# Attention and two expert layers in one kernel: bias moved behind the gather, smaller pieces at the ends of the routing and of the last expert

## Chip, cores and metric

The kernel runs on one core of one Trainium2 chip. The metric is the device time of one execution in microseconds (us). The engines are TensorE (PE in the rows; PEld is its weight load), VectorE (DVE), ScalarE (ACT), GpSimd (POOL) and SyncE (SP), which issues most DMAs. Each engine works through its own queue in order.

## What is computed

The reference, cut to what matters here: an attention over 4 batches and 8 heads with two sparse masks, a dense layer with a squared relu, and a mixture of 8 experts in which every expert gets 288 of the 2304 tokens.

```python
x = attn(q, k, v)                          # 2304 x 512
h = np.maximum(x @ w_in, 0.0)              # 2304 x 2048
x2 = (s * (h * h) + b) @ w_out             # 2304 x 512
logits = x2 @ w_gate                       # 2304 x 8
...                                        # greedy: 288 tokens to each expert
for e in range(8):
    u = np.maximum(x2[mask_e] @ w1[e], 0.0)
    out[mask_e] = u @ w2[e]
```

The scalar bias b reaches x2 as b times the column sums of w_out, one number for each of the 512 columns and the same for every token.

## The kernel before

All matmuls of the dense and expert layers run in a three-pass split: an operand is cut into a high part (a cast) and a low part (what the cast left over), and high x high, high x low and low x high are summed in PSUM.

`mix1` (L590) runs the attention and the first dense layer. Squared relus go to DRAM (`ud`) and come back later. `load_out` (L465) loads w_out, sums its rows in `acc`, and at the end makes from it, with one matmul by ones and one ScalarE activation (L481, L482), a tile `acc` of 128x512 that holds the bias in every partition.

The second dense layer is `x2_late` (L722). It yields after every matmul of 512 columns (L731), so that other code can take them one at a time as filling. `late_step` (L680) loads a block, casts it on ScalarE (L700), subtracts on VectorE (L703) and puts its matmuls into a queue; when a group of 384 tokens is done, `x2_row` (L551) takes each block of 128 tokens out of PSUM with one VectorE operation, which multiplies by s and adds the bias tile (L555), and writes the row to `x2d` in DRAM (L556). There are 18 such rows. The last one is kept apart: its 48 matmuls (`self.tail`, L952) run after the routing.

`route` (L782) finds the experts' tokens in seven rounds of small VectorE steps and small matmuls. Each `yield n` in it lets `run` (L1091) issue n late matmuls before the next step; the numbers are the constants FA0, FA, FB, FP, FC, FK and FE. At the end it builds one-hot tiles (`o96` by L906, `o24` by L908, `w24` by L910 and L911) and gets from 36 small matmuls (L916) the token indices `idx` (L920).

`first_gather` (L940) fetches the first expert's 288 rows with three indirect DMAs on GpSimd, computes meanwhile the last 128 tokens, transposes the rows on TensorE (L958) and adds to them, by a matmul with a "hot" matrix (L963), those rows that only exist in SBUF as yet. `put_x` (L968) then takes one chunk of 96 tokens (four blocks of 96 columns, one for each 128 of the 512 columns, all in one PSUM tile) to `X`: the high part by ScalarE (L971), the low part by VectorE (L972). `gather` (L974) does the same for each later expert: a chunk's DMA in one step, its transposes (L986) three steps later, `put_x` one step after that.

`run` goes through the experts in eight steps each. In a step TensorE runs the second layer (L1023) of the step before last and the first layer (L998) of this step; ScalarE does the relu of the last step (L1004) and two weight casts (L386); VectorE does the relu's low part (L1005) and two weight subtractions (L388). The chunks of the next expert are put in steps 5, 6 and 7, after these. At the end of an expert come the last weight casts and three subtractions, and only then the relu of step 7.

`last_expert` (L1053) computes its second layer token by token (three chunks of 96 tokens, 24 matmuls of 512 columns each, L1061) and writes each chunk with `put`: half a copy on ScalarE (L1067), half on VectorE (L1068), and an indirect DMA on GpSimd to the output (L1069).

Of the kernel before, what the change touches and what calls it, by code (L numbers as in the profile page):

```python
# [74 lines left out]
class Body:  # L75
# [27 lines left out]
    FE = (4, 14, 20)  # L103
# [361 lines left out]
    def load_out(self, fc):  # L465
# [10 lines left out]
        if fc == 15:  # L476
            yield
            yield
            yield
            ps = self.ps()  # L480
            nc.tensor.matmul(ps, self.onesf, self.acc, start=True, stop=True)  # L481
            nc.scalar.activation(self.acc, ps, AF.Copy, scale=self.sb[:, 1:2])  # L482
# [68 lines left out]
    def x2_row(self, g, t, acc):  # L551
# [3 lines left out]
        nc.vector.scalar_tensor_tensor(_two(row), _nat(acc[t]), self.sb[:, 0:1], _two(self.acc), op0=ALU.mult, op1=ALU.add)  # L555
# [226 lines left out]
    def route(self):  # L782
# [66 lines left out]
        for rnd in range(7):  # L849
# [56 lines left out]
        tt(o96, pm.unsqueeze(2).to_broadcast([128, 18, 96]), self.iotaf.unsqueeze(1).to_broadcast([128, 18, 96]),  # L906
           op=ALU.is_equal)
# [4 lines left out]
        yield self.FE[2]  # L912
# [7 lines left out]
        nc.vector.tensor_copy(self.idx, ip[:96, :24])  # L920

# [18 lines left out]
    def first_gather(self):  # L940
# [13 lines left out]
        pss = []  # L954
        for c in range(3):
            ps = self.ps()
            for dc in range(4):
                nc.tensor.matmul(ps[:, dc * 96:(dc + 1) * 96], rows[c][:, dc * 128:(dc + 1) * 128], self.identf[:96, :96],  # L958
                                 start=(dc == 0), stop=False, is_transpose=True, skip_group_check=True)
            pss.append(ps)  # L960
        for c in range(3):
            for dc in range(4):
                nc.tensor.matmul(pss[c][:, dc * 96:(dc + 1) * 96], last[:, dc * 128:(dc + 1) * 128], hot[:, c, :],  # L963
                                 start=False, stop=(dc == 3), skip_group_check=True)
            self.put_x(X, c, pss[c])
        return X

    def put_x(self, X, c, ps):  # L968
        v = ps[:, :384].rearrange("p (d t) -> p d t", d=4)
        h = X[:, 0, :, c * 96:(c + 1) * 96]  # L970
        self.nc.scalar.copy(h, v)  # L971
        self.nc.vector.tensor_tensor(X[:, 1, :, c * 96:(c + 1) * 96], v, _f(h), op=ALU.subtract)  # L972

    def gather(self, e):  # L974
# [3 lines left out]
        def one(c):  # L978
# [9 lines left out]
            self.put_x(X, c, ps)  # L988
# [64 lines left out]
    def last_expert(self, e, X, w1, w2):  # L1053
# [19 lines left out]

        def step(fc):
# [7 lines left out]
            if fc == 7:  # L1082
                put(0)
                for c in (1, 2):
                    for f in range(8):
                        layer2(f, c)
                    put(c)
# [107 lines left out]
```

## Time and profile before

| | us |
|---|---|
| three timed runs, median | 750.45 |
| lowest, highest | 744.54, 750.58 |
| the profiled execution | 745.06 |
| its span, first to last instruction | 743.3 |
| busy in it: TensorE, VectorE, ScalarE, GpSimd | 720.1, 497.9, 374.5, 56.5 |

The profile shows one execution. A row of a timeline gives an instruction's start, its duration, engine, line, output and inputs, and in brackets how long the engine sat idle before it and what released it. Pipelined instructions overlap a little, so the next can start before the recorded end of the last. Attention and the first layer take the first 310 us or so, the second dense layer and the routing go on until 527, the experts until the end.

### The profile page before, as it was taken

What the parts mean: (1) busy time and instruction counts of PE and PEld (TensorE: products, weight loads), DVE (VectorE), ACT (ScalarE), POOL (GpSimd) and SP (SyncE); (2) the same over time, 40 slices, a digit from 0 to 9 for tenths busy, and PEclk for the clock granted to TensorE, in tenths of its full rate; (3) what the DMA queues carried; (4) which work ended last, traced back from release to release, by engine and by line L of the source; (5) the groups of instructions that cost most, each with busy time, mean ns of one, the idle gap of its engine ahead of it and who ended that gap; (6) DMA issues with size and microseconds to landing.
All of it is one profiled execution on the core that took longest, in us unless ns stands there. A gap on an engine that the chain in (4) does not pass through costs nothing.

```text
span 743.3 us, 16623 instructions
## 1 busy us (share of the span) xinstructions
PE 720.1 (97%) x6276; PEld 643.6 (87%) x6276; DVE 497.9 (67%) x1222; ACT 374.5 (50%) x893; POOL 56.5 (8%) x81
## 2 busy tenths in 40 slices
PE   8979999999999999999999998999999999999996
PEld 6769999999999877788778777878999999999994
DVE  6899997987551344478798878794466565666620
ACT  4888776677775655532414221220355555555520
POOL 4000000000000000000000000001112211321211
PEclk9989999999999999999999999999999999999999
DMA  8967756875885899634344423351857767756411
GB/s 234 292 205 224 224 168 210 256 242 193 275 296 192 265 299 296 194 118 154 145 137 148 158 88 117 96 160 60 250 188 236 216 169 239 225 182 191 138 33 32
DMA packets 84655, 140.17 MB, mean 189 GB/s; under 512 B 10848, under 2 KB 44384, under 8 KB 84576
## 3 DMA queue, kind: packets, MB, share of 16 engines
q1 hardware_dynamic: 81504, 129.68, 55.2%
q0 software_dynamic: 3072, 9.44, 3.9%
q8 instruction: 49, 0.80, 0.5%
q14 instruction: 30, 0.25, 0.1%
HBM read 106.32 MB, written 32.77 MB: 187 GB/s over the span
## 4 chain that ended last, share of the span: by engine, by line
PE 82%; DVE 12%; DMA 2%; issue 2%; ACT 0%; SPq 0%; POOLq 0%; DVEq 0%
PE b L501 22%; PE b L731 18%; PE b L998 13%; PE b L1023 11%; PE b L258 2%; PE b L538 2%; PE b L326 2%; PE b L1061 1%; PE b L952 1%; PE b L1039 1%; DVE u L703 1%; DMA r<-ud 1%; PE b L424 1%; DVE wl L388 1%; DVE W L409 1%
## 5 line engine op out<-in xcount | busy, mean ns | idle before, releaser
L731 PE MATMUL b<-wh,u 128*128 128x512 f32 x544 | 168.4, 390 | 1.1 <-DVE u L703 1.1
L731 PEld LDWEIGHTS b<-wh,u 128*128 128x128 f32 x544 | 98.0, 190 | 14.6 <-DVE u L703 1.8
L700 ACT CAST u<-r 128x384 fp32r<-128x384 f32 (+1 forms) x96 | 46.3, 493 | 126.7 <-DMA r<-ud 61.5
L731 PE MATMUL b<-wl,u 128*128 128x512 f32 x272 | 103.3, 380 | 0.0
L1023 PE MATMUL b<-u,wh 128*128 128x288 f32 x448 | 87.9, 293 | 0.0
L501 PE MATMUL b<-xh,wh 128*128 128x384 f32 x384 | 84.0, 341 | 1.1 <-ACT xh L368 1.1
L388 DVE TENSOR_TENSOR wl<-raw,wh 128x512 fp32r<-128x512 f32 x128 | 82.9, 683 | 0.4
L501 PE MATMUL b<-xl,wh 128*128 128x384 f32 x384 | 79.0, 328 | 1.0 <-DVE xl L369 1.0
L386 ACT CAST wh<-raw 128x512 fp32r<-128x512 f32 x128 | 73.3, 618 | 11.1 <-DVE u L703 11.1
L501 PE MATMUL b<-xh,wl 128*128 128x384 f32 x384 | 78.8, 328 | 0.0
L506 ACT ACTIVATE r<-b 128x384 f32<-128x384 f32 x96 | 47.1, 490 | 62.5 <-PE b L501 61.3
L998 PE MATMUL b<-X,wh 128*128 128x288 f32 x512 | 73.4, 286 | 0.6 <-ACT X L971 0.6
L501 PEld LDWEIGHTS b<-xh,wh 128*128 128x128 f32 x384 | 63.0, 191 | 8.7 <-PE b L538 3.1
L1023 PEld LDWEIGHTS b<-u,wh 128*128 128x128 f32 x448 | 69.4, 189 | 0.0
L998 PEld LDWEIGHTS b<-X,wh 128*128 128x128 f32 x512 | 67.4, 189 | 1.3 <-ACT X L971 0.7
L1005 DVE SCALAR_TENSOR_TENSOR u<-b,u 128x288 fp32r<-128x288 f32 x64 | 29.2, 456 | 57.9 <-ACT u L1004 44.6
L501 PEld LDWEIGHTS b<-xl,wh 128*128 128x128 f32 x384 | 65.5, 191 | 1.3 <-DVE xl L369 1.3
L501 PEld LDWEIGHTS b<-xh,wl 128*128 128x128 f32 x384 | 65.4, 190 | 0.2 <-DVE wl L388 0.2
L1023 PE MATMUL b<-u,wl 128*128 128x288 f32 x224 | 64.1, 286 | 0.0
L703 DVE TENSOR_TENSOR u<-r,u 128x384 fp32r<-128x384 f32 (+1 forms) x96 | 47.9, 527 | 15.7 <-ACT u L700 15.6
L731 PEld LDWEIGHTS b<-wl,u 128*128 128x128 f32 x272 | 51.4, 189 | 7.3
L507 ACT ACTIVATE r<-r 128x384 f32<-128x384 f32 x96 | 50.5, 526 | 3.0
(207 smaller groups left out, 1106.4 us busy)
## 6 DMA issues: line engine op xcount, KB each, us to landing
raw<-in_moe_w_dram SPq DMA_DIRECT2D x128, 256.0 KB
r<-ud SPq DMA_DIRECT2D x160, 192.0 KB
ud<-r SPq DMA_DIRECT2D x96, 192.0 KB
raw<-in_words_dram SPq DMA_DIRECT2D x64, 256.0 KB
qk<-in_q_dram SPq DMA_DIRECT2D x24, 288.0 KB
x2d<-E SPq DMA_DIRECT2D x18, 256.0 KB
wod<-K SPq DMA_DIRECT2D x16, 256.0 KB
wo<-wod SPq DMA_DIRECT2D x16, 256.0 KB
```

The lines of the kernel that those rows point to most:

```text
L258: nc.tensor.matmul(sp[64 * j:64 * j + p, c * kw:(c + 1) * kw], qk[sl, 0, q0:q0 + p], qk[sl, 1, k0:k0 + kw], start=after, stop=after or c = ...
L386: nc.scalar.copy(h, W)
L388: nc.vector.tensor_tensor(l, W, _f(h), op=ALU.subtract)
L501: nc.tensor.matmul(ps[:, :self.G], w[:, dc * 128:(dc + 1) * 128], _alt(self.xg[g][dc][x]), start=(k == 0), stop=(k == 11))
L506: nc.scalar.activation(_two(r), _nat(ps[:, :self.G]), AF.Relu)
L507: nc.scalar.activation(r, r, AF.Square)
L700: nc.scalar.copy(d[0], src)
L703: nc.vector.tensor_tensor(d[1], src, _f(d[0]), op=ALU.subtract)
L731: self.nc.tensor.matmul(**args)
L998: self.nc.tensor.matmul(ps[:, :288], w1[dc, fh][wi][:, fs:fs + 128], _alt(X[:, xi, dc, :]), start=(k == 0), stop=(k == 11))
L1005: self.nc.vector.scalar_tensor_tensor(_two(l), _nat(ps[:, :288]), 0.0, _two(_f(h)), op0=ALU.max, op1=ALU.subtract)
L1023: nc.tensor.matmul(y[dc][:, :288], w[:, sl], _alt(u[:, j, :288]), start=(fc == 0 and i == 0), stop=(fc == 7 and i == 2))
```

## The change

- `x2_row` copies on ScalarE, scaled by s, without the bias. `load_out` makes the bias as a tile of 128x4 (a column for each 128 of the 512), by four matmuls of one column.
- `put_x` handles one block of columns and adds the bias there: on ScalarE as the activation's pointer bias, on VectorE as the pointer scalar of a three-operand operation. `gather` calls it four times for a chunk.
- `first_gather` keeps one PSUM tile for each block of 128 columns and 288 tokens in place of one for each chunk of 96 tokens, so the "hot" matmuls are four of 288 columns, and `put_x` takes a quarter of X at a time.
- In `route` the one-hot tile is built in two halves, with five late matmuls issued before each half and before the next tile, and nine before the index matmuls: 24 in place of 20. Two more index columns, `idx2`, address the output in half rows.
- In `last_expert` the third chunk is computed and written in two halves of 256 columns.

```diff
--- before.py
+++ after.py
@@ -100,7 +100,7 @@
     P1S = 28
     A2S = 8
     TM = 2
-    FE = (4, 14, 20)
+    FE = (4, 14, 5, 9)
     P0S = 20
     H0 = (36, 38)
     AE = 2
@@ -478,8 +478,11 @@
             yield
             yield
             ps = self.ps()
-            nc.tensor.matmul(ps, self.onesf, self.acc, start=True, stop=True)
-            nc.scalar.activation(self.acc, ps, AF.Copy, scale=self.sb[:, 1:2])
+            for dc in range(4):
+                nc.tensor.matmul(ps[:, dc:dc + 1], self.acc[:, dc * 128:(dc + 1) * 128], self.onesf[:, :1], start=True,
+                                 stop=True, skip_group_check=True)
+            self.bias = self.c.tile([128, 4], F32, name="bias")
+            nc.scalar.activation(self.bias, ps[:, :4], AF.Copy, scale=self.sb[:, 1:2])
 
     def prep_end(self):
         nc = self.nc
@@ -552,7 +555,7 @@
         nc = self.nc
         i = g * 3 + t
         row = self.Es[i % self.NE].rearrange("p c k -> p (c k)")
-        nc.vector.scalar_tensor_tensor(_two(row), _nat(acc[t]), self.sb[:, 0:1], _two(self.acc), op0=ALU.mult, op1=ALU.add)
+        nc.scalar.activation(_two(row), _nat(acc[t]), AF.Copy, scale=self.sb[:, 0:1])
         nc.sync.dma_start(self.x2d[i * 128:(i + 1) * 128, :], row)
         return row
 
@@ -903,13 +906,17 @@
         stt(pm, ao, -96.0, po, op0=ALU.mult, op1=ALU.add)
         stt(cm, eo, 3.0, ao, op0=ALU.mult, op1=ALU.add)
         o96 = self.xf.tile([128, 18, 96], BF, tag="xb", name="o96")
-        tt(o96, pm.unsqueeze(2).to_broadcast([128, 18, 96]), self.iotaf.unsqueeze(1).to_broadcast([128, 18, 96]),
-           op=ALU.is_equal)
+        for h in range(2):
+            yield self.FE[2]
+            r = slice(9 * h, 9 * h + 9)
+            tt(o96[:, r], pm[:, r].unsqueeze(2).to_broadcast([128, 9, 96]), self.iotaf.unsqueeze(1).to_broadcast([128, 9, 96]),
+               op=ALU.is_equal)
+        yield self.FE[2]
         tt(o24, cm.unsqueeze(2).to_broadcast([128, 18, 24]),
            self.iotaf[:, :24].unsqueeze(1).to_broadcast([128, 18, 24]), op=ALU.is_equal)
         ts(w24[:, 0], o24, self.iotap, None, op0=ALU.mult)
         tt(w24[:, 1], o24, self.iotat.unsqueeze(2).to_broadcast([128, 18, 24]), op=ALU.mult)
-        yield self.FE[2]
+        yield self.FE[3]
         ip = self.ps()
         for i in range(18):
             for k in range(2):
@@ -918,6 +925,9 @@
         self.o96, self.o24 = o96, o24
         self.idx = c.tile([96, 24], I32, name="idx")
         nc.vector.tensor_copy(self.idx, ip[:96, :24])
+        self.idx2 = c.tile([96, 2], I32, name="idx2")
+        for h in range(2):
+            ts(self.idx2[:, h:h + 1], ip[:96, 23:24], 2.0, float(h), op0=ALU.mult, op1=ALU.add)
 
 
     def prep2(self, e, w1, w2):
@@ -951,25 +961,22 @@
         for args in self.tail:
             nc.tensor.matmul(**args)
         last = self.x2_row(self.NG - 1, 2, self.xacc[self.NG - 1])
-        pss = []
-        for c in range(3):
-            ps = self.ps()
-            for dc in range(4):
-                nc.tensor.matmul(ps[:, dc * 96:(dc + 1) * 96], rows[c][:, dc * 128:(dc + 1) * 128], self.identf[:96, :96],
-                                 start=(dc == 0), stop=False, is_transpose=True, skip_group_check=True)
-            pss.append(ps)
+        pss = [self.ps() for _ in range(4)]
         for c in range(3):
             for dc in range(4):
-                nc.tensor.matmul(pss[c][:, dc * 96:(dc + 1) * 96], last[:, dc * 128:(dc + 1) * 128], hot[:, c, :],
-                                 start=False, stop=(dc == 3), skip_group_check=True)
-            self.put_x(X, c, pss[c])
+                nc.tensor.matmul(pss[dc][:, c * 96:(c + 1) * 96], rows[c][:, dc * 128:(dc + 1) * 128], self.identf[:96, :96],
+                                 start=(c == 0), stop=False, is_transpose=True, skip_group_check=True)
+        for dc in range(4):
+            nc.tensor.matmul(pss[dc][:, :288], last[:, dc * 128:(dc + 1) * 128], hot.rearrange("p c t -> p (c t)"),
+                             start=False, stop=True, skip_group_check=True)
+            self.put_x(X, dc, 0, pss[dc][:, :288])
         return X
 
-    def put_x(self, X, c, ps):
-        v = ps[:, :384].rearrange("p (d t) -> p d t", d=4)
-        h = X[:, 0, :, c * 96:(c + 1) * 96]
-        self.nc.scalar.copy(h, v)
-        self.nc.vector.tensor_tensor(X[:, 1, :, c * 96:(c + 1) * 96], v, _f(h), op=ALU.subtract)
+    def put_x(self, X, dc, t, v):
+        h, l = (X[:, i, dc, t:t + v.shape[1]] for i in range(2))
+        bias = self.bias[:, dc:dc + 1]
+        self.nc.scalar.activation(h, v, AF.Identity, bias=bias)
+        self.nc.vector.scalar_tensor_tensor(l, v, bias, _f(h), op0=ALU.add, op1=ALU.subtract)
 
     def gather(self, e):
         nc = self.nc
@@ -985,7 +992,8 @@
             for dc in range(4):
                 nc.tensor.transpose(ps[:, dc * 96:(dc + 1) * 96], t[:, dc * 128:(dc + 1) * 128], self.identf[:96, :96])
             yield
-            self.put_x(X, c, ps)
+            for dc in range(4):
+                self.put_x(X, dc, c * 96, ps[:, dc * 96:(dc + 1) * 96])
 
         return X, (one(c) for c in range(3))
 
@@ -1071,6 +1079,18 @@
                 out_offset=bass.IndirectOffsetOnAxis(ap=self.idx[:, 3 * e + c:3 * e + c + 1], axis=0),
                 in_=t, in_offset=None)
 
+        def half(h):
+            ps = self.ps()
+            for f in range(8):
+                for i, (j, w) in enumerate(((0, 0), (0, 1), (1, 0))):
+                    nc.tensor.matmul(ps[:96, :256], us[f][j][:, 192:288], _alt(w2[f][w][:, 256 * h:256 * h + 256]),
+                                     start=(f == 0 and i == 0), stop=(f == 7 and i == 2))
+            t = self.wt([96, 256], F32, "yh")
+            nc.scalar.copy(_two(t), _nat(ps[:96, :256]))
+            nc.gpsimd.indirect_dma_start(
+                out=self.a["out"].rearrange("n (h d) -> (n h) d", h=2),
+                out_offset=bass.IndirectOffsetOnAxis(ap=self.idx2[:, h:h + 1], axis=0), in_=t, in_offset=None)
+
         def step(fc):
             ps = self.layer1(fc, X, w1)
             yield
@@ -1081,10 +1101,11 @@
             layer2(fc, 0)
             if fc == 7:
                 put(0)
-                for c in (1, 2):
-                    for f in range(8):
-                        layer2(f, c)
-                    put(c)
+                for f in range(8):
+                    layer2(f, 1)
+                put(1)
+                half(0)
+                half(1)
 
         return (step(fc) for fc in range(8))
```

VectorE at the end of the routing, from the last small step on. `o` is the one-hot tile, `u` and `ul` are low parts that the late matmuls need. Before:

```order
L903 SCALAR_TENSOR_TENSOR rt<-rt 128x18
L904 SCALAR_TENSOR_TENSOR rt<-rt 128x18
L906 TENSOR_TENSOR o_6992<-rt,iotaf 128x1728
L908 TENSOR_TENSOR rt<-rt,iotaf 128x432
L910 TENSOR_SCALAR rt<-rt,iotap 128x432
L911 TENSOR_TENSOR rt<-rt,iotat 128x432
L703 TENSOR_TENSOR u_6975<-r_6948,u_6975 128x256
L703 TENSOR_TENSOR ul_6976<-r_6948,ul_6976 128x128
L703 TENSOR_TENSOR u_7001<-r_6965,u_7001 128x256
L703 TENSOR_TENSOR ul_7002<-r_6965,ul_7002 128x128
```

After:

```order
L907 SCALAR_TENSOR_TENSOR rt<-rt 128x18
L706 TENSOR_TENSOR u_6979<-r_6952,u_6979 128x256
L706 TENSOR_TENSOR ul_6980<-r_6952,ul_6980 128x128
L912 TENSOR_TENSOR o_6996<-rt,iotaf 128x864
L706 TENSOR_TENSOR u_7001<-r_6969,u_7001 128x256
L706 TENSOR_TENSOR ul_7002<-r_6969,ul_7002 128x128
L912 TENSOR_TENSOR o_6996<-rt,iotaf 128x864
L915 TENSOR_TENSOR rt<-rt,iotaf 128x432
L917 TENSOR_SCALAR rt<-rt,iotap 128x432
L918 TENSOR_TENSOR rt<-rt,iotat 128x432
```

The four subtractions (L703, now L706) stood behind the whole one-hot work; now two stand ahead of its first half and two between the halves, and the index work is behind all of them.

ScalarE where an expert ends: two weight casts, the last chunk of the next expert's X, two more weight casts, the relu of step 7. In brackets is whose count an instruction waits for. Before:

```order
L1004 ACTIVATE u_1360_7452<-b_7408 128x288 [waits DVE_49,PE_49]
L386 CAST wh_7469<-raw_1355_7425 128x512 [waits DMAHW2_49]
L386 CAST wh_7475<-raw_1358_7431 128x512 [waits DMAHW3_49,DVE_49]
L971 CAST X_7210<-b_7435 128x4x96 [waits PE_49]
L386 CAST wh_7483<-raw_1364_7472 128x512 [waits DMAHW4_49]
L386 CAST wh_7487<-raw_1367_7478 128x512 [waits DMAHW5_49]
L1004 ACTIVATE u_1372_7503<-b_7455 128x288 [waits DVE_49,PE_49]
```

After:

```order
L1012 ACTIVATE u_1361_7467<-b_7417 128x288 [waits PE_49,Activation_49]
L386 CAST wh_7484<-raw_1356_7434 128x512 [waits DMAHW2_49]
L386 CAST wh_7490<-raw_1359_7440 128x512 [waits DMAHW3_49,Activation_49]
L978 ACTIVATE X_7213<-b_7450,bias 128x96 [waits PE_49]
L978 ACTIVATE X_7213<-b_7450,bias 128x96 [waits DVE_49] x3
L386 CAST wh_7504<-raw_1365_7487 128x512 [waits DMAHW4_49]
L386 CAST wh_7508<-raw_1368_7493 128x512 [waits DMAHW5_49]
L1012 ACTIVATE u_1373_7524<-b_7470 128x288 [waits PE_49,Activation_49]
```

One piece that waits for the transposes became four: the first waits for the transposes, each of the other three for VectorE's work on the piece before it.

GpSimd at the end of the program: scatters of finished rows; DMASW is the landing of an earlier scatter or gather. Before:

```order
L1045 DMA out_dram<-yr_9894,idx 2304x512 [waits DMASW2_49,DVE_49]
L1045 DMA out_dram<-yr_9922,idx 2304x512 [waits DMASW4_49,DMASW3_49,Activation_49]
L1069 DMA out_dram<-E_129,idx 2304x512 [waits DMASW4_49,DVE_49]
L1069 DMA out_dram<-E_130,idx 2304x512 [waits DMASW6_49,DMASW5_49,DVE_49]
L1069 DMA out_dram<-E_131,idx 2304x512 [waits DMASW6_49,DVE_49]
```

After:

```order
L1053 DMA out_dram<-yr_10051,idx 2304x512 [waits DMASW4_49,DMASW3_49,Activation_49]
L1077 DMA out_dram<-E_129,idx 2304x512 [waits DMASW4_49,DVE_49]
L1077 DMA out_dram<-E_130,idx 2304x512 [waits DMASW6_49,DMASW5_49,DVE_49]
L1090 DMA out_dram<-yh_10200,idx_7075 4608x256 [waits DMASW6_49,Activation_49]
L1090 DMA out_dram<-yh_10228,idx_7075 4608x256 [waits DMASW7_49,DMASW0_49,Activation_49]
```

One scatter more; each waits, besides its own data, for the landing of the scatter ahead of it.

## Rows read from the trace of the kernel before

**Rows 1.** The page's line of engines: busy us (share of the span) and instructions.

```profile
PE 720.1 (97%) x6276; PEld 643.6 (87%) x6276; DVE 497.9 (67%) x1222; ACT 374.5 (50%) x893; POOL 56.5 (8%) x81
```

**Rows 2.** Busy us of each engine between 600 and 700 us; PE clock, DMA share, GB/s.

```profile
600.00:700.00 100.00, 100.00 (x835) 100.00 (x834) 61.84 (x116) 54.99 (x120) 23.03 (x23) 1.00 0.66 201
```

**Rows 3.** TensorE's waits, 300 to 530 us: total us, times, longest.

```profile
PE b L868 <- DVE rt L862: 3.1, 2, 2.1
PE b L874 <- DVE jc L872: 1.3, 3, 0.7
...
PE b L731 <- DVE u L703: 1.1, 1, 1.1
PE b L998 <- ACT X L971: 0.6, 1, 0.6
```

**Rows 4.** Timeline of VectorE, 446 to 458 us: start, us, instruction [idle before].

```profile
447.82 1.41 DVE L555 SCALAR_TENSOR_TENSOR E<-b,sb,acc 128x512 f32<-128x512 f32 x2 [0.38 <-PE b L731]
...
451.24 0.74 DVE L555 SCALAR_TENSOR_TENSOR E<-b,sb,acc 128x512 f32<-128x512 f32 x1
```

**Rows 5.** Timeline of the routing's end, 503 to 512 us.

```profile
504.63 1.96 DVE L906 TENSOR_TENSOR o<-rt,iotaf 128x1728 bf16<-128x1728 bf16 x1
...
507.39 0.60 DVE L911 TENSOR_TENSOR rt<-rt,iotat 128x432 bf16<-128x432 bf16 x1
...
508.38 0.70 PE L731 MATMUL b<-wh,u 128*128 128x512 f32 x2 [1.10 <-DVE u L703]
```

**Rows 6.** Timeline of TensorE at the first expert's gather.

```profile
523.70 2.92 PE L963 MATMUL b<-hot,E 128*128 128x96 f32 x24
...
527.18 1.35 PE L998 MATMUL b<-X,wh 128*128 128x288 f32 x8 [0.57 <-ACT X L971]
```

**Rows 7.** TensorE groups by form, whole span: shapes, count | busy us, mean ns.

```profile
L538 PE MATMUL b<-r,wog 128*32 128x384 f32 x192 | 18.0, 492 | 0.0
...
L436 PE MATMUL b<-WT,gate 128*32 128x128 f32 x128 | 4.3, 276 | 0.0
```

**Rows 8.** Groups of small shapes and pointer scalars: count | busy us, mean ns.

```profile
L279 ACT ACTIVATE E<-b,nm 128x96 f32<-128x96 f32 x36 | 11.8, 350 | 4.4 <-DVE nm L276 4.4
...
L703 DVE TENSOR_TENSOR ul<-r,ul 128x128 fp32r<-128x128 f32 x16 | 4.5, 284 | 0.0
...
L555 DVE SCALAR_TENSOR_TENSOR E<-b,sb,acc 128x512 f32<-128x512 f32 x18 | 12.9, 741 | 10.2 <-PE b L952 9.2 <-PE b L731 0.9
...
L388 DVE TENSOR_TENSOR wl<-raw,wh 128x512 fp32r<-128x512 f32 x128 | 82.9, 683 | 0.4
```

**Rows 9.** Timeline at the hand-over from one expert to the next, 664 to 684 us.

```profile
668.95 0.41 ACT L1004 ACTIVATE u<-b 128x288 fp32r<-128x288 f32 x1 [1.02 <-PE b L998]
...
675.55 0.41 ACT L1004 ACTIVATE u<-b 128x288 fp32r<-128x288 f32 x1 [1.42 <-PE b L998]
...
676.89 0.48 ACT L971 CAST X<-b 128x384 fp32r<-128x384 f32 x1
...
677.57 0.55 DVE L972 TENSOR_TENSOR X<-b,X 128x384 fp32r<-128x384 f32 x1
678.04 1.89 DVE L388 TENSOR_TENSOR wl<-raw,wh 128x512 fp32r<-128x512 f32 x3
679.84 0.45 DVE L1005 SCALAR_TENSOR_TENSOR u<-b,u 128x288 fp32r<-128x288 f32 x1
...
681.59 0.41 PE L1023 MATMUL b<-u,wh 128*128 128x288 f32 x2
```

**Rows 10.** The end: one row of the chain that ended last, three of the timeline.

```profile
732.40 2.76 DMA out_dram<-E,idx
...
736.48 0.37 ACT L1067 COPY E<-b 96x256 f32<-96x256 f32 x1 [4.81 <-PE b L1061]
736.88 0.42 DVE L1068 COPY E<-b 96x256 f32<-96x256 f32 x1 [4.76 <-ACT E L1067]
737.58 0.92 POOL L1069 DMA_INDIRECT out_dram<-E,idx  x1 [4.26 <-DVE E L1068]
```

## Prediction

> **What bounds the kernel now.** I read the page's engine line first [rows 1]: TensorE is busy 720.1 of a 743.3 us span, the next engine (VectorE) 67%. The reader should take from it that a change gains only where TensorE waits, and loses wherever it makes TensorE wait. So the second view is busy time by stretch [rows 2]: between 600 and 700 us, in the middle of the eight experts, TensorE is busy 100.00 of 100.00 us with 835 matmuls (0.12 us each), ScalarE 55, VectorE 62. There is nothing to gain there, only something to lose. The third view, TensorE's waits from 300 to 530 us [rows 3], shows where there is something: 3.1 and 1.3 us on two steps of the routing (L868, L874), 1.1 us on a VectorE subtraction (L731), 0.6 us on the first expert's X (L998). What follows the last matmul is the third place.
>
> Durations come from one profiled execution: 745.06 us, of which the span is 743.3. The three timed runs have a median of 750.45 and reach from 744.54 to 750.58, so this execution stands at their lower edge. I make the sum against 745.06 and carry the difference over.
>
> **Rows to ScalarE.** The eighteen row copies leave VectorE. In the routing they stand in front of VectorE's own steps [rows 4]: two at 447.82 with a 0.38 us wait for TensorE, one at 451.24, and the next start after a copy comes about 0.08 us before its recorded end, so 0.38 + 1.33 + 0.66 = 2.37 us are in the way of the comparison for which TensorE then waits 2.1 us, the longest of [rows 3]. All of that wait goes. The other waits on L868 and L874 follow row copies too, as far as they are long; of 3.1 + 1.3 us I take 4.2 as gained (bounds 0 and 4.4). ScalarE has room for the copies, so I cost them at nothing there; what waits behind one in ScalarE's queue are the casts of later chunks, which are issued several steps ahead of their matmuls. If that lead were short, the gain would be lost.
>
> **One-hot in pieces.** Now the 1.96 us comparison and three more steps until 507.99 stand in front of the subtractions for which TensorE waits until 508.38 [rows 5]. After the change (first order piece) these come first and between the halves. That wait of 1.1 us goes, but the last step, on which the index matmuls rest, comes later by the time of four subtractions, while only four more matmuls fill it. So a part of the wait reappears at L923. I take a gain of 0.5 (bounds -0.5 and 1.1). The two extra index columns are hidden: the gather also needs the last row written to DRAM.
>
> **First expert by quarters.** Before, from the first "hot" matmul to the first layer-1 matmul it is 527.18 - 523.70 = 3.48 us [rows 6]: 2.92 us for 24 passes, then 0.56 us for the last ScalarE copy. Now there are four matmuls of 288 columns, two passes each. Their price is not in the trace; the slope from 276 ns at 128 columns to 492 ns at 384 [rows 7] is 0.84 ns per column, so 0.24 us a pass, 1.9 us for eight, plus about 0.2 us until the last result is out. (Bounds: 1.0 us at the 0.12 of [rows 2], and the 2.9 us of now.) In the 0.56 us that follow, three matmuls on the first three quarters (0.36 us) already run. So 2.1 + 0.2 = 2.3 us in place of 3.5: gain 1.2 (bounds 0.2 and 2.2).
>
> **The other seven experts: put_x in four pieces.** This is the term that decides. A chunk of 96 tokens left PSUM in one ScalarE cast (0.48 us) and one VectorE subtraction (0.55 us). Now it is four of each, and the second order piece shows that ScalarE's second to fourth pieces wait for VectorE: all four quarters lie in one PSUM tile, and the two engines take turns in it. The same shows in the last chunk's eviction now, where VectorE's copy starts at 736.88, 0.03 us after ScalarE's of the other half ended (736.48 + 0.37) [rows 10]. So a chunk is a chain of eight steps that holds both in-order engines, with 0.03 us at each change of engine.
>
> The Trainium skill (PSUM — Partial Sum Buffer, section on bank collisions) says that two engines must not touch the same bank in the same quadrant at once, reads against reads included. The trace agrees: the 0.42 us copy starts behind the 0.37 us one, not beside it. By a rule of addresses alone the pieces would overlap, and this term would be near nothing.
>
> Price of a piece: the trace has a ScalarE activation of 128x96 from PSUM with a pointer bias, 350 ns [rows 8]. For VectorE, 128x128 without a pointer scalar is 284 ns, so 96 columns some 250; a pointer scalar costs 741 - 683 = 58 ns at 512 columns; I take 310. A round is 0.35 + 0.31 + 2 x 0.03 = 0.72 us. Lower bound: without pointers 0.26 + 0.25 + 0.06 = 0.57. Upper bound: a piece takes no longer than the whole chunk did, 0.48 and 0.55, a round of 1.09; the 350 ns row is much nearer, so I let the upper end stand at 0.90, midway.
>
> Now the chain over three steps of an expert [rows 9]. Say R is the start of a step's ScalarE relu. The chunk's ScalarE cast starts at R + 1.34 (676.89 - 675.55), VectorE's at R + 2.02 (677.57), behind its own relu and two weight splits. With four pieces ScalarE's last ends at R + 2.02 + 3 x 0.72 - 0.03 = R + 4.15, and its next relu can start at R + 4.05. But steps are 3.30 us apart (675.55 - 668.95 is two of them). From 668.95 the next start is at 673.00 and the one after at 677.05, in place of 675.55. VectorE's last piece then ends at 677.05 + 4.15 + 0.03 + 0.31 = 681.54. Behind it stand three weight splits (1.8 us: 678.04 to 679.84 now) and the last relu (0.46), which ends at 683.72. TensorE's second layer needs that relu at 681.59 + 0.12 = 681.71. It waits 2.04 us; part of it, 0.7 us, already at the next expert's X. Now that relu ends at 680.29, 1.4 us ahead, which is all the cover there is. Each 0.1 us on the round makes 0.9 us of wait (nine rounds), so the bounds are 0.7 and 3.7 us. Seven hand-overs from expert to expert: 7 x 2.04 = 14.3 us lost (bounds 5 and 26).
>
> The Trainium skill (ScalarE: Activation LUTs, Rules for kernel authors) budgets about 0.3 us per activation with a pointer bias and 0.83 ns an element: 0.38 us for 96, against the row's 0.35. By it a round is 0.75 us and the term 16.2 us, the sum 1.9 us higher.
>
> **The last chunk in halves.** The third order piece shows that every scatter waits for the one before to land. Now the second lands at 732.40 + 2.76 = 735.16 and the third starts at 737.58, not held up [rows 10]. With halves the first is held until 735.2, some 0.2 us later it starts; at 2.5 us for half the bytes (between half of 2.76, which has fixed parts, and all of it) it lands at 737.9, and the second starts near 738.1, 0.5 us later than now, though its one copy was ready at 737.58 - 0.45 = 737.13. I take a loss of 0.5 less what the smaller transfer gives back: 0.4 (bounds -0.5 and 0.8). The bias matmuls change once and by tenths of a microsecond: nothing.
>
> **Sum.** -4.2 - 0.5 - 1.2 + 14.3 + 0.4 = +8.8 us: 745.06 becomes 753.9, or 750.45 becomes 759.2. Two of three runs lie at 750.5, so I name 758.
>
> **Rivals.**
> First, the other side: the four-piece chain stays covered. If a round costs under about 0.49 us (2.04 / 9 = 0.23 less than mine), VectorE's last relu still comes in time, and only the gains stand: -5.5 us, 739.6 against 745.06, 744.9 against the median. For it speaks that VectorE is idle a third of the time; against it, that the one 128x96 row in the trace makes the ScalarE half alone 0.35. Chance 0.18.
> Second, the pieces cost their lower bound: a round of 0.57 to 0.65 loses 5 to 10 us, the net is between -0.5 and +4, 745 to 755. Chance 0.24.
> Third, the row copies on ScalarE hold up casts, and the routing gains nothing: +13 us, 758 to 764. For it speaks that a copy waits for TensorE in the queue of the engine that feeds it; against it, the idle ScalarE. Chance 0.08.
> The forecast itself, between +5 and +15, has 0.5.
>
> **Numbers.** About 1% (7.5 us) is what a measurement of this kernel can tell from no change. The gains alone are 0.7%, so faster by over 1% needs more than all of them: 0.04. Within 1%: nearly all of the first two rivals and the lower end of the forecast: 0.46. Slower by over 1%: the rest of the forecast and the third rival: 0.50. The range is 744 to 768: its lower end is the first rival on the median's level, its upper the bound of the decisive term cut to what one in ten exceeds. The forecast's own range is 752 to 766.
>
> **What would show it.** Right: in the changed profile TensorE's waits list the second layer's first matmuls (L1031) on VectorE's relu (L1013), seven times about 1.3 us, and layer 1 (L1006) on L978, about 0.7; pieces of 0.35 and 0.31 us in alternation, VectorE's idle put down to ScalarE; L871 and L877 gone from the waits; last scatter some 0.5 us after its copy. Wrong: TensorE busy all through 530 to 720 us, or pieces of ScalarE that overlap VectorE's; then the kernel is a few microseconds faster.

## The result, and the profile after

| | before | after |
|---|---|---|
| median of 6 runs (us) | 746.01 (744.54 to 750.58) | 755.9 (754.76 to 756.83) |
| profiled execution: span (us) | 743.3 | 753.6 |

The change makes the kernel 1.16% slower: the ratio is 1.0116, with a 95% interval of 1.0082 to 1.0151. The prediction was 758.0 us (range 744 to 768) and named slower by over 1% as likeliest. Its sum was +8.8 us; the two medians differ by 9.9 us, the two spans by 10.3 us.

Where the spans part, read off the same events in both timelines (the first of each kind on TensorE, and ScalarE's first yT copy of an expert):

| event | before | after | after minus before | what lies between |
|---|---|---|---|---|
| first transpose of the first gather | 522.69 | 517.44 | -5.25 | routing, one-hot |
| first layer-2 matmul of the first expert | 530.33 | 523.92 | -6.41 | first gather: -1.16 |
| yT of the first expert | 552.56 | 548.30 | -4.26 | one hand-over: +2.15 |
| yT of the seventh expert | 708.08 | 716.80 | +8.72 | six hand-overs: +12.98, 2.16 each |
| end of the span | 743.3 | 753.6 | +10.3 | the last chunk: +1.58 |

So the change earns 6.4 us before the experts and pays 15.1 us in them, and 1.6 us at the end. The changed execution's routing starts 0.83 us later (341.99 in place of 341.16, the first matmul of the same step), behind the attention, which the change hardly touches; without that the gain is 7.2 us and the difference 9.5.

First the busy time in the middle of the experts in the changed kernel (columns as in [rows 2]):

```profile
600.00:700.00 100.00, 95.48 (x762) 92.28 (x761) 64.31 (x137) 58.83 (x141) 22.20 (x22) 1.00 0.63 187
```

It answers to [rows 2]: 100.00 us of TensorE's busy time have become 95.48, with 762 matmuls in place of 835. VectorE and ScalarE are only 2 and 4 us busier; neither is near its limit. TensorE's waits from 520 us to the end say for what it waits (before, 0.6 us in all of this stretch):

```profile
PE b L1031 <- DVE u L1013: 5.6, 7, 0.8
PE b L1006 <- ACT X L978: 2.3, 7, 0.3
```

Seven times each, once per hand-over. The sums are smaller than the loss because the view counts only whole gaps: after one, matmuls start singly as their pieces come. From start to start, the twelve matmuls of layer 1 below take 602.74 - 600.27 = 2.47 us where 1.47 is usual, and the second of the second layer comes 1.18 us behind the first, where 0.12 is usual: 1.00 + 1.06 = 2.06 of the 2.16 us. TensorE's timeline at one hand-over of the changed kernel:

```profile
600.27 0.80 PE L1006 MATMUL b<-X,wh 128*128 128x288 f32 x3
601.40 0.88 PE L1006 MATMUL b<-X,wh 128*128 128x288 f32 x5 [0.34 <-ACT X L978]
602.12 0.65 PE L1006 MATMUL b<-X,wl 128*128 128x288 f32 x4
602.74 0.39 PE L1031 MATMUL b<-u,wh 128*128 128x288 f32 x1
603.92 0.39 PE L1031 MATMUL b<-u,wh 128*128 128x288 f32 x1 [0.79 <-DVE u L1013]
```

And the two engines that make it wait, in the step before (it answers to [rows 9]):

```profile
593.16 0.41 ACT L1012 ACTIVATE u<-b 128x288 fp32r<-128x288 f32 x1
...
597.20 0.40 ACT L1012 ACTIVATE u<-b 128x288 fp32r<-128x288 f32 x1
597.49 1.14 ACT L386 CAST wh<-raw 128x512 fp32r<-128x512 f32 x2
598.52 0.35 ACT L978 ACTIVATE X<-b,bias 128x96 fp32r<-128x96 f32 x1
599.56 0.34 ACT L978 ACTIVATE X<-b,bias 128x96 fp32r<-128x96 f32 x1 [0.68 <-DVE X L979]
600.28 0.34 ACT L978 ACTIVATE X<-b,bias 128x96 fp32r<-128x96 f32 x1 [0.39 <-DVE X L979]
601.01 0.34 ACT L978 ACTIVATE X<-b,bias 128x96 fp32r<-128x96 f32 x1 [0.39 <-DVE X L979]
...
602.28 0.41 ACT L1012 ACTIVATE u<-b 128x288 fp32r<-128x288 f32 x1
```

```profile
599.93 0.32 DVE L979 SCALAR_TENSOR_TENSOR X<-b,bias,X 128x96 fp32r<-128x96 f32 x1 [0.41 <-ACT X L978]
...
601.38 0.32 DVE L979 SCALAR_TENSOR_TENSOR X<-b,bias,X 128x96 fp32r<-128x96 f32 x1 [0.41 <-ACT X L978]
601.62 1.89 DVE L388 TENSOR_TENSOR wl<-raw,wh 128x512 fp32r<-128x512 f32 x3
603.42 0.45 DVE L1013 SCALAR_TENSOR_TENSOR u<-b,u 128x288 fp32r<-128x288 f32 x1
```

Each engine's pieces wait for the other's; a round is 600.28 - 599.56 = 0.72 us. While they take turns, the weight subtractions and VectorE's last relu stand behind them, and that relu is what the second layer waits for.

The routing's waits from 342 to 520 us, which answer to [rows 3], are nearly gone (the first row was there before too, with the same 1.3 us):

```profile
PE b L778 <- DVE rt L895: 1.3, 1, 1.3
...
PE b L877 <- DVE jc L875: 0.2, 1, 0.2
```

The end, GpSimd's rows of the timeline, against [rows 10]:

```profile
741.11 0.92 POOL L1077 DMA_INDIRECT out_dram<-E,idx  x1 [4.26 <-DVE E L1076]
...
744.65 0.92 POOL L1090 DMA_INDIRECT out_dram<-yh,idx  x1 [2.62 <-DMA out_dram<-E,idx]
...
747.80 0.92 POOL L1090 DMA_INDIRECT out_dram<-yh,idx  x1 [2.24 <-DMA out_dram<-yh,idx]
```

From the second chunk's scatter to the last one it was 737.58 - 732.40 = 5.18 us and is 6.69. Each half waits for the landing before it. From the last scatter's start to the end of the span it is 5.70 us before and 5.79 after, so the smaller last transfer gives nothing back.

### The profile page after: what moved, and what is told of

Same layout as the page of the kernel before. It is cut to its first block, busy times and chain, and to the rows that moved or that the text cites. A ratio compares the mean times of both kernels' runs of the same rounds, so it can differ in the third digit from the quotient of the medians.

```text
span 753.6 us, 16785 instructions
## 1 busy us (share of the span) xinstructions
PE 725.8 (96%) x6290; PEld 646.5 (86%) x6290; DVE 501.0 (66%) x1270; ACT 402.4 (53%) x976; POOL 57.6 (8%) x82
## 4 chain that ended last, share of the span: by engine, by line
PE 76%; DVE 10%; DMA 7%; ACT 4%; issue 2%; POOLq 0%; SPq 0%; DVEq 0%; ACTq 0%
PE b L504 26%; PE b L734 20%; PE b L1006 7%; DMA raw<-in_moe_w_dram 6%; PE b L1031 5%; PE b L258 3%; DVE wl L388 3%; PE b L326 2%; PE b L541 2%; ACT wh L386 2%; ACT X L978 1%; PE b L1069 1%; PE b L962 1%; PE b L303 1%; PE b L1047 1%
## 5 line engine op out<-in xcount | busy, mean ns | idle before, releaser
L734 PE MATMUL b<-wh,u 128*128 128x512 f32 x544 | 167.9, 389 | 0.0
L734 PEld LDWEIGHTS b<-wh,u 128*128 128x128 f32 x544 | 98.2, 190 | 12.0 <-issue 1.0
L734 PE MATMUL b<-wl,u 128*128 128x512 f32 x272 | 103.4, 380 | 0.0
L1031 PE MATMUL b<-u,wh 128*128 128x288 f32 x448 | 90.5, 296 | 5.6 <-DVE u L1013 5.6
L703 ACT CAST u<-r 128x384 fp32r<-128x384 f32 (+1 forms) x96 | 46.1, 493 | 79.1 <-DMA r<-ud 30.9
L1006 PE MATMUL b<-X,wh 128*128 128x288 f32 x512 | 77.6, 290 | 2.5 <-ACT X L978 2.3
L734 PEld LDWEIGHTS b<-wl,u 128*128 128x128 f32 x272 | 51.4, 189 | 7.3
L706 DVE TENSOR_TENSOR u<-r,u 128x384 fp32r<-128x384 f32 (+1 forms) x96 | 47.8, 527 | 14.5 <-ACT u L703 14.5
L979 DVE SCALAR_TENSOR_TENSOR X<-b,bias,X 128x96 fp32r<-128x96 f32 (+1 forms) x88 | 28.5, 325 | 38.0 <-ACT X L978 38.0
```

The lines of the kernel that those rows point to most:

```text
L703: nc.scalar.copy(d[0], src)
L706: nc.vector.tensor_tensor(d[1], src, _f(d[0]), op=ALU.subtract)
L734: self.nc.tensor.matmul(**args)
L979: self.nc.vector.scalar_tensor_tensor(l, v, bias, _f(h), op0=ALU.add, op1=ALU.subtract)
L1006: self.nc.tensor.matmul(ps[:, :288], w1[dc, fh][wi][:, fs:fs + 128], _alt(X[:, xi, dc, :]), start=(k == 0), stop=(k == 11))
L1031: nc.tensor.matmul(y[dc][:, :288], w[:, sl], _alt(u[:, j, :288]), start=(fc == 0 and i == 0), stop=(fc == 7 and i == 2))
```

## Experiments

Each diff shows the lines that matter; `...` or a comment stands for the rest.

Two rivals stood against the theory of the turns: that eight small instructions simply cost more than two, and that the hand-overs now wait for the next expert's weights (a weight load has 6% of the chain that ended last).

**e1: the same pieces, not in turns.**

```diff
-            for dc in range(4):
-                self.put_x(X, dc, c * 96, ps[:, dc * 96:(dc + 1) * 96])
+            vs = ...                  # high part, low part, PSUM piece and bias of each quarter
+            for h, l, v, b in vs:
+                nc.scalar.activation(h, v, AF.Identity, bias=b)
+            for h, l, v, b in vs:
+                nc.vector.scalar_tensor_tensor(l, v, b, _f(h), op0=ALU.add, op1=ALU.subtract)
```

> The changed kernel; only the order of the pieces in the later experts' chunks differs: ScalarE's four casts first, then VectorE's four subtractions. The same 84 + 84 instructions, so the same busy time on both engines. Theory (the turns): what costs is that ScalarE's next piece waits for VectorE's and so both in-order engines are held for some 2.9 us of a 3.3 us step. Apart, ScalarE is held some 1.2 us and VectorE 1.3 us; nothing slips from step to step, only the last chunk's subtractions end some 1.5 us later than in the kernel before, which is about the cover of 1.4 us. The waits on L1031 and L1006 all but go (under 0.3 us per hand-over), the time falls from 755.9 by 13 us to about 743. Rival (sheer work: 8 small instructions cost more than 2 large ones, whatever their order): no change, 754 to 757. Rival (weights: the hand-overs wait for the next expert's weights, whose buffers or queue the change delayed): no change either, and the hand-over's wait moves to the weights.

740.02 us, ratio to the kernel before 0.990 (0.9861 to 0.9938); span 738.0. No wait of TensorE is left behind 520 us, and the period from expert to expert is 25.92 us again. The work is the same; VectorE's and ScalarE's busy time between 600 and 700 us even rises against the changed kernel's, since more of the experts' work fits in:

```profile
600.00:700.00 100.00, 100.00 (x837) 100.00 (x835) 68.75 (x153) 61.36 (x155) 23.33 (x23) 1.00 0.63 190
```

Both rivals fall. The time is 3 us below the 743 that was expected: no wait is left at a hand-over, where up to 0.3 us were allowed for. In this kernel's timeline four pieces in a row take 1.04 and 0.99 us, less than the four times 0.34 and 0.32 us of single ones, since on either engine one begins before the last has ended:

```profile
592.21 1.04 ACT L998 ACTIVATE X<-b,bias 128x96 fp32r<-128x96 f32 x4
...
593.29 0.99 DVE L1000 SCALAR_TENSOR_TENSOR X<-b,bias,X 128x96 fp32r<-128x96 f32 x4 [0.31 <-ACT X L998]
```

**e2: whole chunks.**

```diff
-            for dc in range(4):
-                self.put_x(X, dc, c * 96, ps[:, dc * 96:(dc + 1) * 96])
+            self.put_w(X, c, ps)      # one cast, one subtraction, 128x384
```

> The changed kernel, with the chunks of the seven later experts put in one ScalarE cast and one VectorE subtraction as in the kernel before; the bias of these seven experts is left out. Theory (the pieces are the whole loss in the experts): the expert period falls from 28.08 back to 25.92 us, waits on the second layer's first matmuls go, 755.9 - 7 x 2.16 = 740.8 us (739.5 to 742). Rival (part of the loss is elsewhere, in the first expert's quarters or the weights' buffers): a hand-over keeps some tenths of a microsecond, 744 or more.

739.73 us, ratio 0.9892 (0.9854 to 0.993); span 737.6, period 25.92. The pieces are the whole loss in the experts; in e1's order they cost as little as whole chunks.

**e3: only the pieces.** The kernel before, with

```diff
-            self.put_x(X, c, ps)
+            for dc in range(4):       # cast, subtraction, cast, subtraction; h, l, v as in put_x; self.nil is zeros
+                self.nc.scalar.activation(h, v, AF.Identity, bias=self.nil[:, dc:dc + 1])
+                self.nc.vector.scalar_tensor_tensor(l, v, self.nil[:, dc:dc + 1], _f(h), op0=ALU.add, op1=ALU.subtract)
```

> The kernel before, with only the put of the seven later experts' chunks in four pieces each (with pointer biases that are zero here, the bias itself stays in the rows). Theory: 7 x 2.16 = +15.1 us on the kernel before, some 761 us (759 to 763), ratio 1.020, and the same period of 28.08 us from expert to expert. Rival (the loss needs the earlier start of the experts, for instance because weights now come too late for it): the period stays below 27 us and the time below 754.

762.24 us, ratio 1.0199 (1.015 to 1.0247); period 28.10. TensorE's waits from 530 us on are those of the changed kernel:

```profile
PE b L1032 <- DVE u L1014: 5.6, 7, 0.8
PE b L1007 <- ACT X L980: 2.4, 7, 0.3
```

**e4: rows on ScalarE, their bias on GpSimd**, whole chunks, whole last chunk.

```diff
         nc.scalar.activation(_two(row), _nat(acc[t]), AF.Copy, scale=self.sb[:, 0:1])
+        nc.gpsimd.tensor_tensor(row, row, self.acc, op=ALU.add)
         ...                          # last row on VectorE with its bias; put_x without bias
```

> A version that keeps the change's gains and drops what costs: rows leave PSUM on ScalarE without bias and GpSimd adds the bias to the row in SBUF (the very last row on VectorE, scale and bias at once, as before); chunks are put in one cast and one subtraction; the first expert keeps its quarters, without pointer bias; one-hot in pieces; last chunk whole. Theory: the 7.0 us by which the first expert starts earlier stays, the hand-overs cost nothing and the tail nothing: 746.0 - 7.0 = 739 us (737 to 741). If GpSimd's additions slow VectorE or come late for the row's store, the routing's gain of some 5 us is lost in part: 741 to 745.

753.15 us, ratio 1.0074 (1.0045 to 1.0103): a miss, by far more than the 741 to 745 of its bad case. The experts have no wait; the time is lost in the routing, where TensorE waits longer than in [rows 3]:

```profile
PE b L872 <- DVE rt L866: 5.5, 3, 2.8
PE b L878 <- DVE jc L876: 3.6, 4, 1.6
```

VectorE's steps beside the additions show why. In this kernel's timeline, at one of them:

```profile
452.53 0.31 DVE L887 TENSOR_TENSOR rt<-rt 128x144 f32<-128x144 f32 x1
...
452.57 4.01 POOL L559 TENSOR_TENSOR E<-E,acc 128x512 f32<-128x512 f32 x3 [30.97 <-ACT E L558]
...
452.87 1.27 DVE L888 TENSOR_TENSOR rt<-rt 128x144 f32<-128x144 f32 x1
...
454.18 1.27 DVE L889 TENSOR_TENSOR R<-R,rt 128x144 f32<-128x144 f32 x1
...
455.37 1.24 DVE L891 TENSOR_TENSOR rt<-rt 128x8 f32<-128x8 f32 x1
```

A step of 0.31 us (at 428.94 and 429.28, with no addition beside it) takes 1.27 while one runs, and L891, else 0.16, takes 1.24: each nearly as long as one addition (4.01 / 3 = 1.34). Between 342 and 518 us VectorE is busy 146.34 us in all, where e2, without the additions, has 133.52. The Trainium skill (SBUF — State Buffer, section "SBUF: two separate sides") says that a GpSimd operation that reads SBUF and a VectorE instruction with two SBUF inputs exclude each other for the whole of an instruction; these rows agree.

**e5: e1 with the last chunk whole.**

```diff
-                half(0)
-                half(1)
+                for f in range(8):
+                    layer2(f, 2)
+                put(2)
```

> The order of e1 (four casts, then four subtractions) and the last chunk whole again. Theory (each half's scatter waits for the landing before it and about 0.75 us of issue): the 1.5 us that the changed kernel's end lost come back; from the issue of the second chunk's scatter to that of the last it is 5.2 us in place of 6.7; span 738.0 - 1.5 = 736.5, time some 738.5 us, ratio to the kernel before 0.988 to 0.991. Rival (the prediction's size of that term, 0.4): span 737.6.

738.15 us (737.73 to 738.6), ratio 0.9883 (0.9854 to 0.9912); span 736.0. From the second chunk's scatter (725.07) to the last (730.25) it is 5.18 us. This is the fastest kernel of the study, faster than before and after.

**e6 to e8: one part each undone in the changed kernel**, one execution each (762.81, 759.36 and 756.56 us); the first matmul of the first expert, in the changed kernel at 520.22 us, is what is read.

```diff
# e6
-        nc.scalar.activation(_two(row), _nat(acc[t]), AF.Copy, scale=self.sb[:, 0:1])
+        nc.vector.scalar_tensor_tensor(_two(row), _nat(acc[t]), self.sb[:, 0:1], _two(self.acc), op0=ALU.mult, op1=ALU.add)  # self.acc set to zeros
# e7
-        for h in range(2): ...
+        tt(o96, pm..., self.iotaf..., op=ALU.is_equal)      # 128x1728 at once, all 20 late matmuls behind it
# e8
-        pss = [self.ps() for _ in range(4)]      # by quarters
+        for c in range(3): ...                   # by chunks, as before
```

> The changed kernel, but the row copies are again VectorE's, the same instruction as in the kernel before with an added row of zeros (the bias stays behind the gather). Theory (the row copies in front of the routing's own steps): the waits on L871 and L877 come back, 3.1 and about 1.3 us, and the first expert begins 4.2 us later, near 524.4 instead of 520.2 us. Rival (those waits stem from other work, the one-hot or the placing of casts): waits under 1 us, the first expert begins before 521.5. Time +4 over the changed kernel, read from the trace rather than from one time.

The first expert begins at 527.50, 7.28 us later; 0.90 of that is there when the routing starts (342.89 in place of 341.99, a difference in the attention part that I did not follow up), so 6.4 us are the rows', against the 4.2 expected. The two waits of [rows 3] on the routing's steps are back with 3.0 and 1.3 us, and there are more at L779. The rival falls:

```profile
PE b L872 <- DVE rt L866: 3.0, 2, 2.1
...
PE b L878 <- DVE jc L876: 1.3, 3, 0.7
PE b L779 <- DVE sums L774: 1.0, 2, 0.7
PE b L779 <- DVE rt L879: 0.6, 1, 0.6
```

> The changed kernel, but the one-hot comparison is one instruction again, behind it the three others and then 20 fills, as in the kernel before. Theory by the prediction's term: the wait on a subtraction comes back with about 1.1 us, the first expert begins 0.5 to 1.1 us later than 520.2. Rival (the pieces only move the wait): it begins within 0.2 us of 520.2.

It begins at 523.28, 3.06 us later than in the changed kernel, far more than either theory had. 0.26 us are there at the routing's start, 1.10 us are the wait of [rows 5], back again (L734 on L706). Some 2 us behind that wait, in the index matmuls, the granted clock falls: six 128x512 matmuls after them take 510.12 - 507.42 = 2.70 us from start to start where the kernel before takes 512.33 - 510.95 = 1.38, and the second of them starts 0.43 us before the third in place of 0.21, the lower of the two levels (1.2 and 2.4 GHz). Two stretches of e7 (the granted clock stands third from the end), and two rows of its timeline:

```profile
504.00:508.00 4.00, 3.45 (x42) 3.19 (x43) 1.62 (x9) 0.69 (x1) 0.00 (x0) 0.84 0.17 65
508.00:512.00 4.00, 4.00 (x15) 3.33 (x14) 0.29 (x1) 0.69 (x1) 0.00 (x0) 0.73 0.04 15
```

```profile
507.99 0.63 PE L734 MATMUL b<-wl,u 128*128 128x512 f32 x1
508.42 1.06 PE L734 MATMUL b<-wh,u 128*128 128x512 f32 x2
```

By an estimate from the two stretches, 4.00 x (0.16 + 0.27) = 1.7 us are the clock's: 1.3 in the six matmuls and 0.3 in the index matmuls ahead of them (507.42 - 505.52 = 1.90 us, before 510.95 - 509.35 = 1.60). With the 0.26 and the 1.10 that about makes the 3.06. The kernel before had the same wait and kept 1.00 from 504 to 516 us, so the fall does not follow from the wait alone. What else it takes stays open: this was one run.

> The changed kernel, but the first expert's gather is by chunks again (24 matmuls of 96 columns, one cast and one subtraction per chunk); the bias of the first expert is left out. Theory: from the first transpose to the first matmul of the first expert's second layer it is 7.6 us as before, in place of 6.5: 1.2 us later. Rival (the eight matmuls of 288 columns cost as much as the 24): no difference.

Here it is the first stretch that counts: from the first transpose to the first matmul of the second layer it is 524.86 - 517.28 = 7.58 us in place of 523.92 - 517.44 = 6.48: 1.10 us, where 1.2 was expected.

**e9: turns, but two PSUM tiles.**

```diff
-            ps = self.ps()
+            ps = [self.ps() for _ in range(2)]      # transposes and put_x: quarter dc in ps[dc % 2]
```

> The changed kernel with its order of pieces (cast, subtraction, cast, subtraction ...), but the four transposes of a chunk lie in two PSUM tiles, quarters 0 and 2 in one, 1 and 3 in the other; so ScalarE's next piece needs no wait for VectorE's last one. Theory (the turns come from sharing one tile): ScalarE's pieces run beside VectorE's, a chunk takes both engines some 1.7 us instead of 2.9, the hand-overs' waits go, some 741 us (739.5 to 743). Rival (any interleaved order costs, since the engines stand in each other's way in PSUM): pieces still alternate at 0.7 us, 754 to 757. If the second tile runs PSUM short, a wait of TensorE for a free tile shows at the transposes: 743 to 750.

740.43 us, ratio 0.9927 (0.9904 to 0.995), period 25.97; no wait behind 520 us. The order of issue is the changed kernel's, but now pieces of the two engines overlap (ScalarE's from 590.44 to 591.02 with VectorE's from 590.82):

```profile
589.41 0.58 ACT L978 ACTIVATE X<-b,bias 128x96 fp32r<-128x96 f32 x2
...
590.10 0.54 DVE L979 SCALAR_TENSOR_TENSOR X<-b,bias,X 128x96 fp32r<-128x96 f32 x2
...
590.44 0.58 ACT L978 ACTIVATE X<-b,bias 128x96 fp32r<-128x96 f32 x2 [0.45 <-DVE X L979]
...
590.82 0.55 DVE L979 SCALAR_TENSOR_TENSOR X<-b,bias,X 128x96 fp32r<-128x96 f32 x2 [0.18 <-ACT X L978]
```

A chunk is done in 1.96 us (589.41 to 591.37). So the turns need both, the alternating order (e1) and the shared tile.

**e10: e1 with the last of three chunks in turns.**

```diff
+            for p in ([[x] for x in vs] if c == 2 else [vs]):
+                ...                                 # casts of p, then subtractions of p
```

> The kernel of e1, but the third chunk of each later expert is put in turns again, the first two as in e1. Theory by the chain of the prediction: with R the start of ScalarE's relu VectorE's last piece ends at R + 4.5, with the three weight subtractions and the last relu behind it (2.17 us from that end in the changed kernel) it is R + 6.7, needed at R + 6.16: a wait of 0.5 us at L1035 or its like, none at layer 1; 7 x 0.53 = 3.7 us on e1's 740.0, some 743.7 (742.5 to 745). Rival (each chunk in turns costs its share, a third of 15): 745 to 746. Rival (slips must pile up over three chunks before anything is late): 740.

744.75 us, ratio 0.9983 (0.9971 to 0.9994); period 26.59, 0.67 us over e1's (0.53 was expected), and 4.7 us on the whole (3.7). With R = 592.25, VectorE's last piece ends at R + 4.51 and its last relu at R + 6.68, both as expected:

```profile
592.25 0.41 ACT L1017 ACTIVATE u<-b 128x288 fp32r<-128x288 f32 x1 [0.87 <-PE b L1011]
...
596.44 0.32 DVE L1001 SCALAR_TENSOR_TENSOR X<-b,bias,X 128x96 fp32r<-128x96 f32 x1 [0.41 <-ACT X L999]
...
596.67 1.89 DVE L388 TENSOR_TENSOR wl<-raw,wh 128x512 fp32r<-128x512 f32 x3
...
598.48 0.45 DVE L1018 SCALAR_TENSOR_TENSOR u<-b,u 128x288 fp32r<-128x288 f32 x1
```

The wait stands at L1036 alone (2.8 us in seven, as the view counts), none at layer 1: one chunk in turns uses up the cover and 0.67 us more, three make it 2.16. The rival that slips must pile up first falls. By shares, the other rival, it would have been 0.72; the place of the wait, not its size, speaks for the chain.

## Why the prediction was right, point by point

**The pieces: right, in place, size and mechanism.** The term was 7 x 2.04 = 14.3 us; it measured 15.1, and alone (e3) 7 x 2.18 = 15.3 by its period. The round was put at 0.72 us and is 0.72; the relu's start was to slip from R + 3.30 to R + 4.05, and 597.20 - 593.16 is 4.04; VectorE's last relu was to end at R + 6.67, and 603.87 - 597.20 is 6.67. (By the prediction's own rows the wait is 683.72 - 681.71 = 2.01, not 2.04; seven times that is 14.1.) Of what the measured 2.16 has over it, 0.1 us lies in the first matmul after the wait (603.92 to 604.15, 0.23 us in place of 0.12). The split between the two waits was off: 0.7 of 2.04 us was put at layer 1, where 1.0 of 2.16 stands; and the view shows 0.8 and 0.3 us a time, not 1.3 and 0.7, since it counts whole gaps. The budget of the Trainium skill (ScalarE: Activation LUTs, Rules for kernel authors) for an activation with a pointer bias, 0.38 us by the prediction's working, would have made the term 16.2; the pieces measure 0.342 us on the mean in the changed kernel.

For the rule that the prediction cites from the Trainium skill (PSUM — Partial Sum Buffer, section on bank collisions), that two engines must not touch one bank in one quadrant at once, the runs show this much: in one tile the engines take turns (after), in two they overlap (e9). Whether the chip would forbid it in one tile was not tried: the trace shows a wait on the other engine's instruction, which the program sets.

**Rows to ScalarE: right in kind, too small.** 4.2 us were predicted, with a bound of 4.4; undone, it costs 6.4. The step that failed is the count of what goes: I counted the waits on L868 and L874 alone. Undoing the rows in the changed kernel brings 1.0 and 0.6 us of waits at the prefix (L779), where the changed kernel and the kernel before have 0.2 (beside 1.3 us that all three have). Not all of that is the rows' for certain: e3, whose routing is the kernel before's, has the longest of them, 0.7 us, as well in its execution, so that one comes and goes between executions:

```profile
PE b L775 <- DVE sums L770: 1.0, 2, 0.7
```

The waits of e6 exceed the changed kernel's by 5.5 us in all; what makes the other 0.9 of the 6.4 stays open. The parts do not add up: rows and one-hot together gave 5.25 us by the timelines, 6.1 if the 0.83 us by which the changed kernel's routing starts later is taken off.

**One-hot in pieces: too small.** I let a part of the 1.1 us wait reappear at the index matmuls and took 0.5. They start straight behind their fills, and take 2.00 us in place of the 1.75 of the kernel before, so 0.25 us reappeared:

```profile
504.71 2.00 PE L923 MATMUL b<-rt,o 128*96 128x24 bf16 x36
```

When it was undone the 1.1 us came back whole, and behind it a fall of the clock that the kernel before did not have.

**First expert by quarters: right.** Predicted 1.2, measured 1.16 between the kernels and 1.10 alone. The eight passes take 520.22 - 518.44 = 1.78 us; 1.9 were predicted from the slope of [rows 7]. Layer 1 then starts at once, against the 0.57 us of waiting in [rows 6]; its first eight matmuls take 521.96 - 520.22 = 1.74 us, before 528.37 - 527.18 = 1.19, as the quarters come one by one:

```profile
518.44 2.16 PE L970 MATMUL b<-hot,E 128*128 128x288 f32 x8
520.22 1.91 PE L1006 MATMUL b<-X,wh 128*128 128x288 f32 x8
```

**Last chunk in halves: right in kind, 0.4 predicted, 1.5 measured.** The step that failed is "some 0.2 us later it starts": from a landing (741.11 + 2.75 = 743.86) to the next scatter's start it is 0.79 us, and 0.80 the second time. Twice 0.6 us more, less the 0.15 by which half the bytes land sooner than taken (2.35 us, not 2.5), is 1.0 of the 1.1 us that were missed; the rest is the 0.1 us that the smaller transfer was to give back and did not. So the last scatter starts 2.2 us behind the end of its copy (747.80 against 745.25 + 0.37), not 0.5.

So the sum of +8.8 missed the spans' 10.3 by 1.5: gains of 6.4 (predicted 5.9), pieces 15.1 (14.3), end 1.6 (0.4). That the gains agree so well is partly luck: without the later start of the routing they are 7.2. The absolute 758.0 came out 2 us high because it leaned on the median of three runs of before, 750.45; that of six is 746.01, and from there the sum gives 754.8, 1.1 low, so two errors of opposite sign helped it. That the change came out on the far side of 1% was close as well: the chances were 0.50 against 0.46, and the interval of the ratio begins at 1.0082.

The first rival (the chain stays covered) needed a round under 0.49 us, the second one of 0.57 to 0.65; both fall with 0.72. The third (row copies on ScalarE hold up casts) falls with the missing waits in the routing.

## What to carry to other kernels

When two in-order engines each read the same tile in pieces, look at the order in which the pieces are written: piece by piece, each engine waits for the other and both are held for the sum of all pieces; all of one engine's first, or every other piece in another tile, cost next to nothing here (740.02 and 740.43 us, against 739.73 with whole chunks). Price such an edit not by busy time but by the next instruction that stands behind the pieces on each engine, and by how long its reader can wait; here 1.4 us of cover stood against 0.75 us of slip per step, three steps long. A split last transfer lost 1.5 us here, since its pieces wait for one another's landing; one whose pieces need not wait was not tried.

## What I had not expected of the hardware

GpSimd's 128x512 additions in SBUF stretched VectorE's steps with two SBUF inputs from 0.31 to 1.27 us (e4); as a helper for VectorE it cost more than it took over (ratio 1.0074). An indirect scatter that waits for the one before starts 0.79 to 0.80 us after its landing, and half the bytes save only 0.4 us of 2.75. Behind a wait of 1.1 us the granted clock fell in one kernel (e7: 0.84 and 0.73, some 1.7 us by the estimate above) and stayed at 1.00 in another.
